# Values' high and low part as one stationary block of 128 columns, weights split at a later place, float32 products in eight steps instead of twenty-four

## The chip, the cores and the metric

The kernel runs on one core of a Trainium2 chip. The metric is device time in microseconds (us) of one launch, the median of the runs. Engines are called PE (TensorE's matmuls), PEld (its loads of the stationary operand), DVE (VectorE), ACT (ScalarE), POOL (GpSimd) and SP (the queue that issues the DMAs).

## The reference, cut to what matters

Local attention with a window of 32 and 32 global tokens, over 8 batches and 8 heads, then a two-layer network with 2048 hidden units over all 4352 rows. All of it is in float32.

```
s_g = scale * q_g @ k_all.T ;  out_g = softmax(s_g) @ v_all        # 32 global queries, all 544 keys
s_l = scale * [q_l @ k_g.T, mask(q_l @ k_l.T)]                     # 512 local queries, |i - j| <= 32
out_l = softmax(s_l) @ [v_g, v_l]
x = concat(out_g, out_l)  as 4352 rows of 512
h = x @ w_in ;  g = h * sigmoid(h) ;  out = g @ w_out              # w_in 512 x 2048, w_out 2048 x 512
```

The weights come as 64-bit floats and are turned to float32 on the chip.

## The kernel before

**Precision.** A float32 product is either given to PE as it is (one instruction, which the trace shows as two matmul records), or as three products of halves: a value x is split into a high part (a rounded copy in the format fp32r, made on ACT) and a low part (x minus the high part, made on DVE or POOL), and PE adds high x high, high x low and low x high in PSUM.

**Attention** runs in 128 steps: 8 batches b, 4 chunks c of 128 queries, 4 pairs of heads; step k does one pair for one chunk. A step loads queries and keys (`st_load`) and values (`st_vload`), splits them (`st_split`, `st_vsplit`), makes scores on PE and the softmax on DVE and ACT (`st_scores`), turns the probabilities by four PE transposes and splits them into `pt_hi` and `pt_lo` (`st_turn`), and multiplies them with the values into one PSUM bank `o` (`st_out`). Behind the 128 probabilities of the local queries `pt` holds 32 columns of the global queries (copied on POOL), so these matmuls are 160 wide for the first half a of the keys, and for the second half 128, except in the last chunk, where it is 160. For each of two heads u, a split step does six matmuls with a stationary block of 64 columns: pt_hi with vhi and with vlo for both halves a, then pt_lo with vhi for both. ACT and DVE then move the result out: xh and xl (high and low) for the local rows, and an addition to `acc` for the global rows. Steps k below KF use whole float32 (no splits, no DMA of the probabilities); below ND POOL makes the low parts of keys and values, from ND on DVE. Global scores and softmax of the next batch go in between (`g_*`): their 544 probabilities are brought by DMA into an fp32r tile (`g_move`), turned and kept in `pgt`.

**The network** runs in 12 blocks n of two or three tiles of 128 rows (SIZES). For each of 16 slices f of the hidden units: `first_layer` makes h, tanh and the split of g, `second_layer` of the slice before adds to the output tiles. Block 0 works in whole float32 while the weights are still being converted (`load_weights`: DMA, ACT line 179, DVE lines 181 and 182); `split_weights` makes their high parts on ACT (line 192) and low parts on POOL (line 193) for the blocks from 1 on.

**Order.** PE's order is the order of the code: a stream of attention parts with due times is advanced by `fill` between the network's matmuls, so the steps k = 8 to about 22 lie in block 0. The other engines and the DMA queue take an order that a list scheduler made; every engine works its list strictly in order. `keep_in_program_order` holds the first eight loads of weights (those of f = 0 to 3) at their place among the loads.

Of the kernel before, what the change touches and what calls it, by code (L numbers as in the profile page):

```python
# [39 lines left out]
ND = 28  # L40
KF = 24
GF = 2
KP = 12
SCRATCH = 8
LOOK = 5
FIRSTW, PACE, WAT = 2, 1.0, -1.5

# [11 lines left out]
def attention_moe_kernel(ctx: ExitStack, tc: tile.TileContext, qk0_in, qk_in, v_in, gqk, wts, out):  # L59
# [154 lines left out]
    def g_scores(b, p):  # L214
        did(("scores", b, p), *([("turn" if b <= GF else "move", b - 1, p // 2)] if b else []))
        rows = slice(QG * (p % 2), QG * (p % 2 + 1))
# [35 lines left out]
    def g_move(b, hh):  # L252
        did(("move", b, hh), ("soft", b, hh))
        if b < GF:
            return
        r0 = two.tile([P, 4 * P], F32R, tag="o", name=f"rg0_{b}_{hh}")
        r1 = two.tile([P, SG], F32R, tag="rg", name=f"rg1_{b}_{hh}")
        nc.sync.dma_start(out=r0.bitcast(F32), in_=pgs[hh][:, : 4 * P])
        nc.sync.dma_start(out=r1.bitcast(F32), in_=pgs[hh][:, 4 * P :])
        state["rg", hh] = r0, r1  # L260

    def g_turn(b, hh):
        whole = b < GF
        if whole:
            r0, r1, idt = pgs[hh], pgs[hh][:, 4 * P :], ident.bitcast(F32)
        else:
            (r0, r1), idt = state.pop(("rg", hh)), ident
        did(("turn", b, hh), ("turn", b, 0) if hh else ("last", b - 1))
        if hh == 0:
            state["pgt"] = work.tile([P, 5, H, SG], F32, tag="pgt", name=f"pgt{b}")  # L270
        pgt = state["pgt"]
# [5 lines left out]
        nc.scalar.copy(out=pgt[:, 0:4, hs, :], in_=tb.rearrange("p (t h q) -> p t h q", t=4, h=4))  # L277
# [15 lines left out]
    def st_vload(k, b, c, pr):  # L293
        if k < KF and k % 2:
            vraw = two.tile([P, 2, 2, D], F32, tag="vhi" if k % 4 == 1 else "vlo", name=f"vraw{k}")
# [20 lines left out]
    def st_vsplit(k, b, c, pr):  # L316
        if k < KF:
            return
        vraw = tiles.pop(("vraw", k))
        vhi = two.tile([P, 2, 2, D], F32R, tag="vhi", name=f"vhi{k}")  # L320
        vlo = two.tile([P, 2, 2, D], F32R, tag="vlo", name=f"vlo{k}")
        nc.scalar.copy(out=vhi, in_=vraw)
        (nc.gpsimd if k < ND else nc.vector).tensor_tensor(
            out=vlo, in0=vraw, in1=vhi.bitcast(F32), op=ALU.subtract)
        tiles["v", k] = vhi, vlo

# [41 lines left out]
    def st_turn(k, b, c, pr):  # L368
# [7 lines left out]
        for i in range(4):  # L376
# [3 lines left out]
            nc.tensor.transpose(t[:, i * P : (i + 1) * P].bitcast(F32R), rr[:, i * P : (i + 1) * P], ident)  # L380
        t4 = t.rearrange("p (u a q) -> p u a q", u=2, a=2)
        if whole:
            pt = tiles["pt", k] = pt_whole(k)
            if c == NC - 1:
                nc.gpsimd.memset(pt[:, :, 1, P:], 0.0)
            nc.scalar.copy(out=pt[:, :, :, :P], in_=t4)
        else:
            pt_hi, pt_lo = pt_tiles(k)
            nc.scalar.copy(out=pt_hi[:, :, :, :P], in_=t4)
            nc.vector.tensor_tensor(out=pt_lo[:, :, :, :P], in0=t4, in1=pt_hi[:, :, :, :P].bitcast(F32),  # L390
                                    op=ALU.subtract)
        did(("last", b) if (c, pr) == (NC - 1, NPR - 1) else k, ("turn", b, pr // 2))
        pgt = state["pgt"]
        for a in range(2 if c == NC - 1 else 1):
            n = P if a == 0 else SG
            g = pgt[:n, c + a, 2 * pr : 2 * pr + 2, :]
            if whole:
                nc.gpsimd.tensor_copy(out=pt[:n, :, a, P:], in_=g)
                continue
            nc.gpsimd.tensor_copy(out=pt_hi[:n, :, a, P:], in_=g)  # L400
            nc.gpsimd.tensor_tensor(out=pt_lo[:n, :, a, P:], in0=g, in1=pt_hi[:n, :, a, P:].bitcast(F32),
                                    op=ALU.subtract)

    def st_out(k, b, c, pr, t):
# [4 lines left out]
        if whole:  # L409
            vraw, pt_f = tiles.pop(("vraw", k)), tiles.pop(("pt", k))  # L410
        else:
            vhi, vlo = tiles.pop(("v", k))
            pt_hi, pt_lo = pt_tiles(k)
        o = attbank("o", f"o{k}")
        wide = P + SG
        for u in range(2):
            if whole:
                terms = [(vraw, pt_f, a) for a in range(2)]
            else:
                terms = [(v, pt_hi, a) for a in range(2) for v in (vhi, vlo)] + [(vhi, pt_lo, a) for a in range(2)]  # L420
            for i, (v, pt, a) in enumerate(terms):
                m = wide if a == 0 or c == NC - 1 else P
                nc.tensor.matmul(o[:D, u * wide : u * wide + m], v[:, a, u, :], pt[:, u, a, :m],  # L423
                                 start=(i == 0), stop=(i == len(terms) - 1))
        g0 = SG * (b % 4)
        for u in range(2):
            rows = slice(D * u, D * (u + 1))
            src = o[:D, u * wide : u * wide + P]
            if n == 0 and u == 0:
                nc.scalar.copy(out=xh[rows, pr, sl], in_=src)  # L430
            elif n == 0:
                nc.vector.tensor_copy(out=xh[rows, pr, sl], in_=src)
            else:
                nc.scalar.copy(out=xh[rows, pr, sl], in_=src)  # L434
                nc.vector.tensor_tensor(out=xl[rows, pr, sl], in0=src, in1=xh[rows, pr, sl].bitcast(F32),  # L435
                                        op=ALU.subtract)
            gsrc = o[:D, u * wide + P : (u + 1) * wide]
            gdst = acc[rows, pr, g0 : g0 + SG]
            if c == 0:
                nc.vector.tensor_copy(out=gdst, in_=gsrc)  # L440
            else:
                nc.vector.tensor_tensor(out=gdst, in0=gsrc, in1=gdst, op=ALU.add)

# [135 lines left out]
    def second_layer(n, f, gh, gl):  # L579
# [3 lines left out]
        for i, o in enumerate(outs[n]):  # L583
# [7 lines left out]
            fill(1)  # L591
        if n == 0:
            split_weights(f)
        if f == NF - 1:
# [11 lines left out]
    for n in range(len(SIZES)):  # L606
        for f in range(NF):
# [81 lines left out]
```

## Time and profile before

| | |
|---|---|
| time, median of 3 runs | 1088.51 us (1087.3 to 1088.69) |
| the profiled execution's own time | 1086.34 us |
| its span | 1084.6 us |
| busy: PE, PEld, DVE, ACT, POOL | 97%, 86%, 67%, 64%, 14% |
| matmul records, instructions in all | 6568, 20466 |
| mean granted clock of TensorE | 0.989 of full |

Matmuls overlap in the trace: a record of a 384-wide one is 0.34 us long, but the next begins 0.17 us after it. What a matmul costs in a full queue is therefore read from start to start, and the row behind a run of short ones is read with it.

### The profile page before, as it was taken

To read this page: it belongs to the slowest core of one execution; us is meant where nothing else is said; L and a number is where in the kernel's file an instruction comes from. 1 tells how busy PE (TensorE), PEld (TensorE's weight loads), DVE (VectorE), ACT (ScalarE), POOL (GpSimd) and SP (SyncE) were. 2 spreads that over 40 slices of the span, in tenths; PEclk is the share of its full clock that TensorE was granted. 3 is DMA by queue.
4 is the path that set the end of the run, shared out by engine and by line. 5 is a ranking of instruction groups with operands and counts; after the bars stand their busy time and mean duration, and the time that the engine had idled before them with its cause. 6 is when DMAs were issued, how large, how long until landed. Compare 5 with 4: busy or idle time off the path is not lost.

```text
span 1084.6 us, 20466 instructions
## 1 busy us (share of the span) xinstructions
PE 1053.5 (97%) x6568; PEld 934.9 (86%) x6568; DVE 727.4 (67%) x2367; ACT 693.0 (64%) x1845; POOL 146.5 (14%) x360
## 2 busy tenths in 40 slices
PE   6878999999999999999999999999999999999998
PEld 4645778989999999999999999998999999999997
DVE  5974355777677777666777877786778867753322
ACT  7875456767677766656766766776677776653232
POOL 3123542111100110000110100001000111000000
PEclk8989999999999999999999999999999999999999
DMA  9961112343334333332433433443344433310000
GB/s 351 380 189 59 57 59 76 119 146 125 111 112 142 124 107 115 116 115 82 140 110 122 149 111 109 138 135 108 111 141 125 141 114 112 112 60 20 1 30 20
DMA packets 69611, 127.29 MB, mean 117 GB/s; under 512 B 9344, under 2 KB 29312, under 8 KB 69504
## 3 DMA queue, kind: packets, MB, share of 16 engines
q1 hardware_dynamic: 69504, 125.99, 36.1%
q8 instruction: 52, 0.85, 0.3%
q14 instruction: 55, 0.45, 0.1%
HBM read 86.44 MB, written 8.91 MB: 88 GB/s over the span
## 4 chain that ended last, share of the span: by engine, by line
PE 93%; ACT 3%; DVE 2%; issue 1%; DMA 1%; ACTq 0%; DVEq 0%
PE h L563 33%; PE out L588 12%; PE out L590 11%; PE out L589 11%; PE o L423 10%; PE s L345 6%; PE t L380 3%; PE h L557 2%; PE out L586 2%; PE t L378 1%; DMA raw_w<-in_wts_dram 1%; PE gs L226 1%; PE gs L228 1%; ACT w_hi L192 1%; ACT w L179 1%
## 5 line engine op out<-in xcount | busy, mean ns | idle before, releaser
L563 PE MATMUL h<-xh,w_hi 128*128 128x384 f32 (+1 forms) x704 | 236.8, 336 | 0.0
L563 PE MATMUL h<-xh,w_lo 128*128 128x384 f32 (+1 forms) x704 | 233.5, 332 | 0.0
L563 PE MATMUL h<-xl,w_hi 128*128 128x384 f32 (+1 forms) x704 | 233.1, 331 | 0.0
L569 ACT ACTIVATE t<-h 128x384 f32<-128x384 f32 (+1 forms) x192 | 90.7, 472 | 207.3 <-PE h L563 189.4
L588 PE MATMUL out<-w_hi,gh 128*128 128x512 f32 x512 | 210.6, 411 | 0.0
L590 PE MATMUL out<-w_hi,gl 128*128 128x512 f32 x512 | 201.3, 393 | 0.0
L589 PE MATMUL out<-w_lo,gh 128*128 128x512 f32 x512 | 200.3, 391 | 0.0
L571 DVE SCALAR_TENSOR_TENSOR t<-t,h 128x384 f32<-128x384 f32 (+1 forms) x176 | 95.2, 541 | 132.6 <-ACT t L569 131.9
L563 PEld LDWEIGHTS h<-xl,w_hi 128*128 128x128 f32 x704 | 132.6, 188 | 5.4 <-issue 0.5
L563 PEld LDWEIGHTS h<-xh,w_hi 128*128 128x128 f32 x704 | 132.5, 188 | 5.4 <-issue 0.7
L400 POOL CAST pt_hi<-pgt 128x64 fp32r<-128x64 f32 (+1 forms) x132 | 39.1, 308 | 724.4 <-PE o L423 706.1
L563 PEld LDWEIGHTS h<-xh,w_lo 128*128 128x128 f32 x704 | 132.3, 188 | 0.0
L576 DVE TENSOR_TENSOR gl<-t,gh 128x384 fp32r<-128x384 f32 (+1 forms) x176 | 96.8, 550 | 46.6 <-PE out L590 42.5
L349 DVE CUSTOM_DVE_ANT_0 probs<-s,mask 128x224 f32<-128x224 f32 x244 | 85.0, 384 | 62.0 <-PE s L345 61.4
L353 ACT ACTIVATE probs<-probs,st 128x224 f32<-128x224 f32 x244 | 115.7, 475 | 11.2 <-DVE st L349 10.5
L590 PEld LDWEIGHTS out<-w_hi,gl 128*128 128x128 f32 x512 | 96.1, 188 | 22.3 <-DVE gl L576 0.3
L589 PEld LDWEIGHTS out<-w_lo,gh 128*128 128x128 f32 x512 | 97.0, 189 | 10.5
L588 PEld LDWEIGHTS out<-w_hi,gh 128*128 128x128 f32 x512 | 96.4, 188 | 10.6 <-ACT gh L575 0.4
L575 ACT CAST gh<-t 128x384 fp32r<-128x384 f32 (+1 forms) x176 | 88.3, 501 | 21.8 <-DVE t L571 17.3
L434 ACT CAST xh<-o 64x128 fp32r<-64x128 f32 x240 | 61.3, 256 | 42.5 <-PE o L423 29.4
L312 ACT CAST qk<-raw 128x704 fp32r<-128x704 f32 x100 | 78.2, 782 | 15.9 <-PE s L345 15.6
L435 DVE TENSOR_TENSOR xl<-o,xh 64x128 fp32r<-64x128 f32 x240 | 67.3, 280 | 30.9 <-ACT xh L434 27.4
(117 smaller groups left out, 1937.3 us busy)
## 6 DMA issues: line engine op xcount, KB each, us to landing
raw<-in_qk_dram SPq DMA_DIRECT2D x100, 352.0 KB, 3.0
rr<-probs SPq DMA_DIRECT2D x104, 256.0 KB, 2.3
raw_w<-in_wts_dram SPq DMA_DIRECT2D x32, 512.0 KB, 6.3
vraw<-in_v_dram SPq DMA_DIRECT2D x128, 128.0 KB, 2.4
raw_g<-in_gqk_dram SPq DMA_DIRECT2D x32, 304.0 KB, 2.9
out_dram<-o SPq DMA_DIRECT2D x32, 256.0 KB, 2.3
raw<-in_qk_dram SPq DMA_DIRECT2D x28, 240.0 KB, 4.8
rg<-pg SPq DMA_DIRECT2D x12, 256.0 KB, 2.4
```

The source lines that it names most:

```text
L312: nc.scalar.copy(out=qk, in_=raw)
L349: nc.vector.tensor_tensor_reduce(out=p[:, u, :W], in0=s[:, u * W : (u + 1) * W], in1=mask_of[c], scale=-SCALE, scalar=3.0e38, op0=ALU.add, ...
L353: nc.scalar.activation(p[:, u, :W], p[:, u, :W], AF.Exp, bias=st[:, u : u + 1], scale=-1.0, accum_out=st[:, 2 + u : 3 + u])
L423: nc.tensor.matmul(o[:D, u * wide : u * wide + m], v[:, a, u, :], pt[:, u, a, :m], start=(i == 0), stop=(i == len(terms) - 1))
L563: nc.tensor.matmul(h[:, :nt], wt, x[:, c, :nt], start=(i == 0), stop=(i == 3 * NCC - 1))
L569: nc.scalar.activation(t[:, :nt], h[:, :nt], AF.Tanh, scale=0.5)
L571: nc.vector.scalar_tensor_tensor(out=out[:, :nt], in0=t[:, :nt], scalar=1.0, in1=h[:, :nt], op0=ALU.add, op1=ALU.mult)
L575: nc.scalar.copy(out=gh[:, :nt], in_=t[:, :nt])
L576: nc.vector.tensor_tensor(out=gl[:, :nt], in0=t[:, :nt], in1=gh[:, :nt].bitcast(F32), op=ALU.subtract)
L588: nc.tensor.matmul(o, gh[:, sl], wh, start=(f == 0), stop=False)
L589: nc.tensor.matmul(o, gh[:, sl], wl, start=False, stop=False)
L590: nc.tensor.matmul(o, gl[:, sl], wh, start=False, stop=(f == NF - 1))
```

## The change

What it does, part by part. In a split step vhi and vlo become the two halves of one tile `vv`, so that one stationary block of 128 columns (vhi then vlo) is multiplied with pt_hi; the product lands in 128 partitions, high part in the first 64 and low part in the others. A step does eight matmuls in place of twelve. ACT copies the upper 64 partitions to a tile `xs`, DVE adds the lower 64, for each u; then ACT and DVE make xh and xl over 128 partitions in one instruction each, and POOL adds the global rows to `acc`. KF goes from 24 to 8: steps 8 to 23 are split steps now. The weights are no longer split after each slice of block 0 but by a count: the first at slice 7 of block 0, then one for each 0.75 slice. FIRSTW goes from 2 to 4: four instead of six halves of weights are asked for ahead of block 0. The last 32 probabilities of the global queries are turned as float32 straight from `pgs` (no second DMA) into two small tiles `pgh` and `pgl`.

```
-KF = 24
+KF = 8
+SPLIT0, SPLITS = 7, 0.75
-FIRSTW, PACE, WAT = 2, 1.0, -1.5
+FIRSTW, PACE, WAT = 4, 1.0, -1.5
...
         tb = attbank("s", f"gu{b}_{hh}")
-        nc.tensor.transpose(tb[:SG, :P] if whole else tb[:SG, :P].bitcast(F32R), r1, idt)
-        nc.scalar.copy(out=pgt[:SG, 4, hs, :], in_=tb[:SG, :P].rearrange("p (h q) -> p h q", h=4))
+        nc.tensor.transpose(tb[:SG, :P], pgs[hh][:, 4 * P :], ident.bitcast(F32))
+        for i in range(2):
+            rows, src = slice(SG * (2 * hh + i), SG * (2 * hh + i + 1)), tb[:SG, QG * i : QG * (i + 1)]
+            nc.scalar.copy(out=pgh[rows, :], in_=src)
+            nc.vector.tensor_tensor(out=pgl[rows, :], in0=src, in1=pgh[rows, :].bitcast(F32), op=ALU.subtract)
...
-        vhi = two.tile([P, 2, 2, D], F32R, tag="vhi", name=f"vhi{k}")
-        vlo = two.tile([P, 2, 2, D], F32R, tag="vlo", name=f"vlo{k}")
+        vv = two.tile([P, 2, 2, 2, D], F32R, tag="vv", name=f"vv{k}")
+        vhi, vlo = vv[:, :, :, 0, :], vv[:, :, :, 1, :]
...
         for u in range(2):
-                terms = [(v, pt_hi, a) for a in range(2) for v in (vhi, vlo)] + [(vhi, pt_lo, a) for a in range(2)]
...
+                nc.tensor.matmul(o[:, at], vv[:, a, u].rearrange("p t d -> p (t d)"), pt_hi[:, u, a, :m],
+                                 start=(a == 0), stop=(a == 1))
+                nc.tensor.matmul(o[:D, at], vv[:, a, u, 0], pt_lo[:, u, a, :m], start=False, stop=(a == 1),
+                                 skip_group_check=(a == 1))
...
-                nc.scalar.copy(out=xh[rows, pr, sl], in_=src)
-                nc.vector.tensor_tensor(out=xl[rows, pr, sl], in0=src, in1=xh[rows, pr, sl].bitcast(F32),
-                                        op=ALU.subtract)
...
-                nc.vector.tensor_tensor(out=gdst, in0=gsrc, in1=gdst, op=ALU.add)
+            nc.scalar.copy(out=xs[rows, :], in_=o[D:, at])
+            nc.vector.tensor_tensor(out=xs[rows, :], in0=o[:D, at], in1=xs[rows, :], op=ALU.add)
+        nc.scalar.copy(out=xh[:, pr, sl], in_=xs[:, :P])
+        nc.vector.tensor_tensor(out=xl[:, pr, sl], in0=xs[:, :P], in1=xh[:, pr, sl].bitcast(F32), op=ALU.subtract)
+        if c == 0:
+            nc.gpsimd.tensor_copy(out=gdst, in_=xs[:, P:])
+        else:
+            nc.gpsimd.tensor_tensor(out=gdst, in0=xs[:, P:], in1=gdst, op=ALU.add)
...
-        if n == 0:
-            split_weights(f)
...
+            while len(w_hi) < NF and SPLIT0 + SPLITS * len(w_hi) <= NF * n + f:
+                split_weights(len(w_hi))
             g = first_layer(n, f)
```

**PE, the values of step 30.** Before, twelve matmuls into 64 partitions (a name's first number is the step, `x2` stands for two rows):

```order
L423 MATMUL o30_2489<-pt_hi_1795,vhi30_2383 64x160
L423 MATMUL o30_2489<-pt_hi_1795,vlo30_2384 64x160
L423 MATMUL o30_2489<-pt_hi_1795,vhi30_2383 64x160
L423 MATMUL o30_2489<-pt_hi_1795,vlo30_2384 64x160
L423 MATMUL o30_2489<-pt_lo_1797,vhi30_2383 64x160 x2
```

These are the six of head u = 0, and the same six follow for u = 1. Now there are four for each head:

```order
L430 MATMUL o30_2801<-pt_hi_555,vv30_2701 128x160
L432 MATMUL o30_2801<-pt_lo_557,vv30_2701 64x160
L430 MATMUL o30_2801<-pt_hi_555,vv30_2701 128x160
L432 MATMUL o30_2801<-pt_lo_557,vv30_2701 64x160
L430 MATMUL o30_2801<-pt_hi_555,vv30_2701 128x160
```

The two with vlo are gone, and the blocks of 128 and of 64 columns alternate; PE's order around them is the same as before.

**POOL, in block 0, from the global rows of step 12 to those of step 13**, as it is now (`w_lo5` is the low part of the weights of slice 5, `klo` and `vv` are low parts of keys and values, `acc` the sum of the global rows):

```order
L458 TENSOR_TENSOR acc_125<-xs12_1016,acc_125 128x32
L315 TENSOR_TENSOR klo16_1164<-raw16_1093,qk16_1163 128x480
L194 TENSOR_TENSOR w_lo5_1379<-w5_630,w_hi5_1378 128x512 x2
L400 CAST pt_hi_555<-pgt0_202 128x2x32
L406 COPY pt_hi_555<-pgh0_203 32x2x32
L406 COPY pt_lo_557<-pgl0_204 32x2x32
L328 TENSOR_TENSOR vv15_1207<-vraw15_1086,vv15_1207 128x4x64
L194 TENSOR_TENSOR w_lo6_1450<-w6_697,w_hi6_1449 128x512 x2
L315 TENSOR_TENSOR klo17_1249<-raw17_1179,qk17_1248 128x480
L401 TENSOR_TENSOR pt_lo_557<-pgt0_202,pt_hi_555 128x2x32
L458 TENSOR_TENSOR acc_125<-xs13_1105,acc_125 128x32
```

Before, POOL's list in this stretch had the weights and small copies for `pt` alone:

```order
L193 TENSOR_TENSOR w_lo4_877<-w4_545,w_hi4_876 128x512 x2
L385 MEMSET pt13_975 128x2x32
L398 COPY pt13_975<-pgt0_208 128x2x32
L398 COPY pt13_975<-pgt0_208 32x2x32
L385 MEMSET pt14_1043 128x2x32
```

So the low parts of keys and values of steps 8 to 23 now stand between the weights, and the splits of the weights are still in block 0.

**ACT, ahead of the first tanh of block 0** (`t0_0`), as it is now: the turn of step 8 and conversions of weights 2, 3 and 6 stand directly before it.

```order
L314 CAST qk11_690<-raw11_628 128x480
L362 ACTIVATE probs1__117<-probs1__117,st9_524 128x224
L180 ACTIVATE w2_563<-raw_w2_0_564 128x512
L180 ACTIVATE w2_563<-raw_w2_512_569 128x512
L193 CAST w_hi2_1192<-w2_563 128x512
L180 ACTIVATE w3_574<-raw_w3_0_575 128x512
L193 CAST w_hi2_1192<-w2_563 128x512
L193 CAST w_hi3_1290<-w3_574 128x512
L180 ACTIVATE w3_574<-raw_w3_512_580 128x512
L397 CAST pt_hi_555<-t8_550 128x4x128
```

Three rows follow (a cast of w3 and two conversions of w6) before `t0_0`. Before, the rows ahead of it were these:

```order
L353 ACTIVATE probs1__117,st9_506<-probs1__117,st9_506 128x224
L430 COPY x_0_299<-o7_515 64x128
L353 ACTIVATE probs1__117,st9_506<-probs1__117,st9_506 128x224
L386 COPY pt8_531<-t8_526 128x4x128
L179 ACTIVATE w12_1015<-raw_w12_0_1016 128x512
L569 ACTIVATE t0_0_561<-h0_0_556 128x256
```

Counted over the two whole lists, 18 conversions (line 179) and 6 casts of weights (line 192) stood ahead of `t0_0` before, and 22 and 12 stand there now, with 4 casts of queries and keys and 2 of values that were not there. The transpose of step 8 needs its probabilities by DMA now, which is issued after the loads of the weights of slices 2 and 3.

## Rows read from the trace of the kernel before

**Rows 1.** Windows: from:to, length, busy of PE, PEld, DVE, ACT, POOL, clock, DMA share, GB/s
```profile
40.00:60.00 20.00, 15.53 (x83) 11.54 (x84) 17.37 (x60) 17.07 (x45) 1.58 (x4) 0.99 0.92 331
...
140.00:160.00 20.00, 20.00 (x97) 14.76 (x95) 11.92 (x38) 9.88 (x28) 9.28 (x10) 1.00 0.16 45
...
300.00:400.00 100.00, 99.99 (x667) 91.88 (x666) 76.26 (x250) 70.76 (x190) 10.77 (x34) 1.00 0.40 126
```

**Rows 2.** Waits of PE, whole span: us in total, times, longest
```profile
PE o L423 <- issue: 6.6, 5, 3.2
...
PE gs L226 <- DVE acc L442: 3.3, 1, 3.3
PE o L423 <- ACT pg L231: 2.7, 1, 2.7
```

**Rows 3.** Timeline of PE, a split step's twelve value matmuls: start, length
```profile
326.47 0.24 PE L423 MATMUL o<-pt_hi,vhi 128*64 128x160 f32 x1
...
327.28 0.45 PE L588 MATMUL out<-w_hi,gh 128*128 128x512 f32 x1
327.57 0.39 PE L589 MATMUL out<-w_lo,gh 128*128 128x512 f32 x1
327.80 0.39 PE L590 MATMUL out<-w_hi,gl 128*128 128x512 f32 x1
```

**Rows 4.** Timeline of PE, four transposes with 128 stationary columns, and what follows
```profile
608.59 0.46 PE L380 MATMUL t<-ident,rr 128*128 128x128 f32 x4
608.88 0.46 PE L588 MATMUL out<-w_hi,gh 128*128 128x512 f32 x1
609.19 0.39 PE L589 MATMUL out<-w_lo,gh 128*128 128x512 f32 x1
```

**Rows 5.** Timeline of PE, four score matmuls of 224 with 128 stationary columns
```profile
328.03 0.27 PE L345 MATMUL s<-qk 128*128 128x224 f32 x1
...
328.46 0.35 PE L563 MATMUL h<-xh,w_hi 128*128 128x384 f32 x1
```

**Rows 6.** Timeline of PE, a float32 step's values (step 23) and what follows
```profile
182.01 1.19 PE L423 MATMUL o<-pt,vraw 128*64 128x160 f32 x8
183.13 0.37 PE L345 MATMUL s<-qk 128*128 128x224 f32 x1
183.34 0.27 PE L345 MATMUL s<-klo,qk 128*128 128x224 f32 x1
```

**Rows 7.** Timeline of PE, the values of steps 12 and 18 in block 0
```profile
100.04 1.27 PE L423 MATMUL o<-pt,vraw 128*64 128x160 f32 x8 [0.51 <-issue]
...
144.19 1.19 PE L423 MATMUL o<-pt,vraw 128*64 128x160 f32 x8
```

**Rows 8.** Groups by line: POOL's, count, busy us, mean ns, idle before
```profile
L193 POOL TENSOR_TENSOR w_lo<-w,w_hi 128x512 fp32r<-128x512 f32 x32 | 41.1, 1304 | 47.5 <-PE out L586 29.6 <-ACT w_hi L192 17.8
L400 POOL CAST pt_hi<-pgt 128x64 fp32r<-128x64 f32 (+1 forms) x132 | 39.1, 308 | 724.4 <-PE o L423 706.1 <-ACT probs L353 18.1 <-ACT probs L357 0.2
L310 POOL TENSOR_TENSOR klo<-raw,qk 128x480 fp32r<-128x480 f32 x4 | 4.9, 1214 | 11.4 <-ACT qk L309 11.4
L323 POOL TENSOR_TENSOR vlo<-vraw,vhi 128x256 fp32r<-128x256 f32 x4 | 3.3, 818 | 2.6 <-ACT vhi L322 2.6
```

**Rows 9.** Groups by line: ACT's and DVE's moves of a step's result, and the weights' conversion
```profile
L435 DVE TENSOR_TENSOR xl<-o,xh 64x128 fp32r<-64x128 f32 x240 | 67.3, 280 | 30.9 <-ACT xh L434 27.4 <-PE out L586 0.4
L434 ACT CAST xh<-o 64x128 fp32r<-64x128 f32 x240 | 61.3, 256 | 42.5 <-PE o L423 29.4 <-DVE acc L442 4.1 <-DVE acc L440 4.0
L442 DVE TENSOR_TENSOR acc<-o,acc 64x32 f32<-64x32 f32 x192 | 33.3, 173 | 0.2
L179 ACT ACTIVATE w<-raw_w 128x512 f32<-128x512 f32 x32 | 21.3, 667 | 3.4 <-DMA raw_w<-in_wts_dram 3.2
L192 ACT CAST w_hi<-w 128x512 fp32r<-128x512 f32 x32 | 18.5, 614 | 4.8 <-DVE w L182 3.5 <-PE s L345 1.3
```

**Rows 10.** Timeline of ACT, the first tanh of block 0
```profile
49.96 0.38 ACT L569 ACTIVATE t<-h 128x256 f32<-128x256 f32 x1 [0.43 <-PE h L557]
```

More of the change, by code (lines that the diff above doesn't have):

```diff
@@ L214, in g_scores @@
     def g_scores(b, p):
-        did(("scores", b, p), *([("turn" if b <= GF else "move", b - 1, p // 2)] if b else []))
+        did(("scores", b, p), *([("turn", b - 1, p // 2)] if b else []))
         rows = slice(QG * (p % 2), QG * (p % 2 + 1))
@@ L256, in g_move @@
         r0 = two.tile([P, 4 * P], F32R, tag="o", name=f"rg0_{b}_{hh}")
-        r1 = two.tile([P, SG], F32R, tag="rg", name=f"rg1_{b}_{hh}")
         nc.sync.dma_start(out=r0.bitcast(F32), in_=pgs[hh][:, : 4 * P])
-        nc.sync.dma_start(out=r1.bitcast(F32), in_=pgs[hh][:, 4 * P :])
-        state["rg", hh] = r0, r1
+        state["rg", hh] = r0
     def g_turn(b, hh):
@@ L294, in st_vload @@
         if k < KF and k % 2:
-            vraw = two.tile([P, 2, 2, D], F32, tag="vhi" if k % 4 == 1 else "vlo", name=f"vraw{k}")
+            vraw = two.tile([P, 2, 2, 2, D], F32, tag="vv", name=f"vraw{k}")[:, 0]
         else:
@@ L415, in st_out @@
         wide = P + SG
+        gdst = acc[:, pr, SG * (b % 4) : SG * (b % 4 + 1)]
         for u in range(2):
-            if whole:
-                terms = [(vraw, pt_f, a) for a in range(2)]
-            else:
-                terms = [(v, pt_hi, a) for a in range(2) for v in (vhi, vlo)] + [(vhi, pt_lo, a) for a in range(2)]
-            for i, (v, pt, a) in enumerate(terms):
-                m = wide if a == 0 or c == NC - 1 else P
-                nc.tensor.matmul(o[:D, u * wide : u * wide + m], v[:, a, u, :], pt[:, u, a, :m],
-                                 start=(i == 0), stop=(i == len(terms) - 1))
@@ L425, in st_out @@
-        g0 = SG * (b % 4)
+            for a in range(2):
+                m = wide if a == 0 or c == NC - 1 else P
+                at = slice(u * wide, u * wide + m)
+                if whole:
+                    nc.tensor.matmul(o[:D, at], vraw[:, a, u, :], pt_f[:, u, a, :m], start=(a == 0), stop=(a == 1))
+                    continue
+                nc.tensor.matmul(o[:, at], vv[:, a, u].rearrange("p t d -> p (t d)"), pt_hi[:, u, a, :m],
+                                 start=(a == 0), stop=(a == 1))
+                nc.tensor.matmul(o[:D, at], vv[:, a, u, 0], pt_lo[:, u, a, :m], start=False, stop=(a == 1),
+                                 skip_group_check=(a == 1))
@@ new lines, in st_out @@
+        if n == 0:
+            for u in range(2):
+                rows = slice(D * u, D * (u + 1))
+                src, gsrc = o[:D, u * wide : u * wide + P], o[:D, u * wide + P : (u + 1) * wide]
+                if u == 0:
+                    nc.scalar.copy(out=xh[rows, pr, sl], in_=src)
+                else:
+                    nc.vector.tensor_copy(out=xh[rows, pr, sl], in_=src)
+                if c == 0:
+                    nc.vector.tensor_copy(out=gdst[rows, :], in_=gsrc)
+                else:
+                    nc.vector.tensor_tensor(out=gdst[rows, :], in0=gsrc, in1=gdst[rows, :], op=ALU.add)
+            return
@@ L426, in st_out @@
+        xs = work.tile([P, wide], F32, tag="xs", name=f"xs{k}")
         for u in range(2):
+            at = slice(u * wide, (u + 1) * wide)
             rows = slice(D * u, D * (u + 1))
-            src = o[:D, u * wide : u * wide + P]
-            if n == 0 and u == 0:
-                nc.scalar.copy(out=xh[rows, pr, sl], in_=src)
[L431 to L434, printed above, removed]
-                nc.vector.tensor_tensor(out=xl[rows, pr, sl], in0=src, in1=xh[rows, pr, sl].bitcast(F32),
-                                        op=ALU.subtract)
```

57 lines of the change are left out of this document (28 added, 29 removed).

## The prediction

> **What bounds the kernel now.** I read the windows first [rows 1]. In block 0's second half and in the middle PE has no gap: it is busy for 20.00 of 20 us and for 99.99 of 100, at full clock, while DVE is busy 76% and ACT 71% in the middle. There the time is PE's own work, and whatever is taken from PE comes off the end, as long as nobody else becomes late. At the start it is different: between 40 and 60 us PE is busy 15.5 of 20, DVE 17.4 and ACT 17.1, and the DMA engines are 92% full. That is the stage in which the weights arrive and are converted. The waits of PE [rows 2] lie nearly all in it: 6.6 us in which value matmuls wait for something the profile doesn't name, 3.3 us behind a DVE addition that holds the bank `o`, 2.7 us behind ACT. Then I read PE's timeline from start to start, since the records overlap.
>
> **Values, 104 steps that were split before.** The twelve matmuls begin at 326.47, the next matmul at 327.28, so 0.81 us [rows 3]. The matmul behind them then needs 0.29 where the one after it needs 0.23: 0.06 us of the run comes due there. Together 0.87 us, or 73 ns each. Eight instead of twelve at the same price would be 0.58. But four of the eight now have a stationary block of 128 columns. The nearest row is the four transposes, 128 columns stationary and 128 moving [rows 4]: 0.29 us to the next matmul, which then takes 0.31 instead of 0.23, so 0.37 us, or 92 ns each. So a step is 4 x 92 + 4 x 73 = 0.66 us and saves 0.21; 104 steps save 22 us. The bounds: if the wider block costs nothing, 0.87 - 0.58 = 0.29 a step, 30 us; if it costs as much as a score matmul with 128 stationary and 224 moving columns, 0.43 us for four or 108 ns each [rows 5], then 4 x 108 + 4 x 73 = 0.72, 0.15 a step, 15 us. I take the transposes, because their moving side is as short as here.
>
> The Trainium skill, page "TensorE: Matmul & The Clock Gate", section "LDWEIGHTS (loading the stationary operand)", says that a load takes the number of stationary columns divided by 1.2 GHz, whatever the rows: 107 ns for 128 columns and 53 ns for 64. By it alone the four wide ones would cost 107 ns each and the saving would be near 15 us, an estimate from that page. The transposes' 92 ns do not agree with it, the scores' 108 ns would.
>
> **Moving the result.** Before, a step has two ACT casts of 256 ns, two DVE subtractions of 280 and two additions of 173 [rows 9]. Now there are two ACT copies and two DVE additions of 64 x 160, an ACT cast and a DVE subtraction of 128 x 128, and a small POOL addition. Taking each as the nearest row, ACT goes from 0.51 to 0.77 us and DVE from 0.91 to 0.84, or a little more since 160 is wider than 128. For ACT that is 0.26 us a step in steps of some 8 us, 3% more on 71% [rows 1]: hidden, PE does not wait for ACT there. The bank `o` was passed from ACT to DVE to ACT to DVE before and is now, so its release costs nothing new. If that cover is gone, the price is the rival below.
>
> **Steps 8 to 23.** A float32 step's values take 1.12 us to the next matmul, which takes 0.21 where its like take 0.11 [rows 6, 5]: 1.22 us. As a split step it is 0.66: 0.56 less. The transposes and scores are about equal in both forms; I put 0.6 on the whole. Twelve of these steps (12 to 23) begin at 100 us or later [rows 7], where PE is the bound: at most 7 us. But POOL gets new work. With the rows of POOL [rows 8], from the global rows of step 12 to those of step 18 its list now holds nine pairs of weights' low parts (9 x 2.61), seven of keys (7 x 1.21), six of values (6 x 0.82) and 30 small operations of 0.31 at most: 23.5 + 8.5 + 4.9 + 9.3 = 46 us, perhaps 43 as many of the small ones are smaller than the row. PE took 144.19 - 100.04 = 44.2 us for the same six steps [rows 7] and would now want 40.6. So POOL holds this stretch at about what it was, and only steps 18 to 23, where two pairs of weights are left, give their 0.6 each: 4 us. I take 4; bounds 0 and 7.
>
> **The start.** Ahead of the first tanh of block 0 ACT now has 4 more conversions of weights (667 ns), 6 more casts of weights (614 ns) [rows 9], and 6 casts of keys and values that are new, bounded by those 614 ns: 2.7 + 3.7 + 3.7 = 10 us more on an engine that has no room there [rows 1]. The weights' part, 6.4 us, is not new work, only earlier: all 32 conversions and casts are done by about the same place of block 0, so it comes back there. What stays is the new casts, 3 us. Also late: the transpose of step 8 now waits for a DMA that is issued behind four loads of weights, and in the in-order list of ACT the first tanh stands behind it. I put the start at 3 us later; bounds: 10 us (nothing comes back), and 3 us earlier (two of the waits of [rows 2] go).
>
> The later split of weights changes nothing by itself: the scheduler still puts the high parts as early as before, and the low parts are done before block 1 needs them. One transpose per half batch as float32, and twelve DMAs less, are below what can be told.
>
> **Sum.** -22 - 4 + 3 = -23 us. From the profiled execution's own 1086.3 that gives 1063; the median of the runs stands 2 us above that execution, so about 1065; I say 1064.
>
> **Rivals.**
> - *The wide load binds.* The blocks of 128 columns are loaded more slowly than the short moving side runs, at 108 ns as in [rows 5]: -15 - 4 + 3 = -16 us, 1072. For it: no row shows a wide load behind a narrow one, and the scores are the dearest that there is; against: their moving side is longer than here, and the transposes take 92 ns. The page of the Trainium skill named above gives the same. 12%.
> - *POOL and the weights hold the start longer.* The DMAs of the probabilities of steps 8 to 11 stand in the one load queue behind loads of weights that wait for buffers, and each transpose waits; the start's 10 us stay and block 0 gains nothing: -22 + 10 = -12, 1076. For it: the order of the queue. Against: in the old run PE waits there anyway, for the same weights. 10%.
> - *More than thought.* The wide block costs nothing, POOL keeps up, the waits of 3.3 and 2.7 us go: -30 - 7 - 3 = -40 us, 1048. 12%.
> - *Slower.* One ACT list holds the copies of `o`, and its second copy waits for DVE's first addition. Behind it stand the tanh and the cast of g, for which the second layer waits. If that costs PE 0.22 us in each of 120 steps, the 26 us of the values and of block 0 are gone; at 0.35 us it is 42 - 23 = 19 us more, 1108. For it: DVE is 76% busy, so the addition queues. Against: the old chain has the same alternation, and PE waits for none of it between 300 and 400 us. 4%.
> - *No change*, where two of these meet half-way: 2%.
>
> **How the numbers follow.** The forecast as summed, 1053 to 1071 with the bounds of its three terms moved singly, has 60%. The range 1050 to 1077 takes in it, the wide load, most of the slow start and about a third of the case of more. 0.2% is 2 us, about what a measurement of this kernel can tell from no change: faster 94%, same 2%, slower 4%.
>
> **What the changed profile would show.** In the middle, PE still without a gap; eight value matmuls taking 0.6 to 0.66 us to the next one, with 60 to 75 ns behind a block of 64 columns and up to 92 ahead of one of 128. In block 0, POOL busy more than 9 of 10 us between steps 12 and 18, with PE waiting for `pt_lo` or for the low part of the values. The first tanh of block 0 near 58 us instead of 50 [rows 10], with most of these 8 us won back by step 12. I am wrong if PE shows waits for ACT or DVE in each step behind 200 us, or if the values' run is as long as before.

## The result and the profile after

The changed kernel takes **1093.5 us** (median; 1091.8 to 1093.9), the one before 1088.5 beside it: ratio 1.0044, 95% interval 1.0028 to 1.006. It is slower; the prediction said 1064 and 94% for faster. One of its five executions took 3509.7 us, three times the others, and is left out of the range and the ratio. The profiled execution has a span of 1091.6 us, 7.1 more than before's. First the page's span and engine shares:

```profile
span 1091.6 us, 20153 instructions
PE 1036.8 (95%) x6184; PEld 923.3 (85%) x6184; DVE 768.1 (70%) x2295; ACT 750.9 (69%) x2013; POOL 225.5 (21%) x528
```

The windows, columns as in [rows 1]:

```profile
40.00:60.00 20.00, 10.71 (x55) 8.68 (x53) 12.57 (x39) 12.88 (x32) 7.07 (x12) 0.67 0.59 197
...
120.00:140.00 20.00, 16.49 (x91) 12.07 (x91) 14.37 (x37) 12.15 (x37) 18.16 (x25) 1.00 0.30 94
140.00:160.00 20.00, 16.96 (x87) 12.53 (x86) 12.88 (x32) 10.97 (x33) 14.85 (x21) 0.91 0.25 76
...
300.00:400.00 100.00, 99.75 (x624) 91.70 (x624) 78.36 (x242) 75.36 (x205) 16.07 (x47) 1.00 0.41 125
```

In the middle PE still has no gap. The stage that changed is the start: between 40 and 60 us every engine is *less* busy than in [rows 1] except POOL, and the DMA engines moved 197 GB/s instead of 331. The next view says what PE waits for. The waits of PE, whole span, columns as in [rows 2]:

```profile
PE t L385 <- DMA rr<-probs__116: 11.7, 1, 11.7
PE gs L227 <- DVE xs L452: 6.2, 2, 3.1
PE o L426 <- issue: 4.8, 4, 2.3
PE s L350 <- DVE pgl L285: 4.3, 3, 3.0
```

One wait is 11.7 us long. On the timeline of PE (start, length, in brackets the idle time before) it is the transposes of step 8:

```profile
46.23 0.54 PE L350 MATMUL s<-qk 128*128 128x224 f32 x1
46.57 0.41 PE L350 MATMUL s<-klo,qk 128*128 128x224 f32 x1
46.78 0.41 PE L350 MATMUL s<-qk,klo 128*128 128x224 f32 x1
...
49.42 0.35 PE L350 MATMUL s<-qk 128*128 128x224 f32 x1
...
49.72 0.28 PE L350 MATMUL s<-qk,klo 128*128 128x224 f32 x1
49.83 0.27 PE L350 MATMUL s<-qk 128*128 128x224 f32 x1
...
50.81 1.17 PE L426 MATMUL o<-pt,vraw 128*64 128x160 f32 x8 [0.49 <-issue]
63.66 0.72 PE L385 MATMUL t<-ident,rr 128*128 128x128 f32 x4 [11.68 <-DMA rr<-probs__116]
64.18 2.03 PE L573 MATMUL h<-x,w 128*128 128x256 f32 x4
```

The reader should see the order: the scores of steps 8 and 9 (46.23 and 49.42), the values of step 7 (50.81), the transposes of step 8 (63.66), and only behind them the first slice of block 0 (64.18; the expectations below call the network's slices expert slices). That slice needs nothing of step 8, but it stands behind it on PE's list. The timeline of SP, the one queue from which loads and copies are issued:

```profile
44.62 0.33 SPq L172 DMA_DIRECT2D raw_w<-in_wts_dram  x1
49.10 0.33 SPq L303 DMA_DIRECT2D vraw<-in_v_dram  x1
...
52.34 2.14 SPq L172 DMA_DIRECT2D raw_w<-in_wts_dram  x4
54.60 0.70 SPq L370 DMA_DIRECT2D rr<-probs__116  x1
```

Between 44.95 and 49.10 SP issues nothing: its next load waits for the buffer that a values run of PE still reads. Then four halves of weights go out at once, 512 KB each, and the copy for step 8 goes out behind them at 54.60. The DMA view from 40 to 70 us says when it lands (KB each, us from issue):

```profile
raw_w<-in_wts_dram SPq DMA_DIRECT2D x10, 512.0 KB, 5.5
...
rr<-probs__116 SPq DMA_DIRECT2D x1, 256.0 KB, 8.9
```

54.6 + 8.9 = 63.5, and PE goes on at 63.66. (From 100 us on, the copies land in 2.3 us by the median.)

A second cost stands beside the waits: TensorE's granted clock. In these traces it is at one of two levels, 1.2 GHz (0.50 in the windows) and 2.4 GHz (1.00). PE had stood still since 51.98 when the clock fell at 54.80, and it stayed low to 68.5, so the transposes of step 8 and the first slice ran at the lower level. Two windows, columns as in [rows 1]:

```profile
54.80:63.66 8.86, 0.00 (x1) 0.03 (x1) 3.88 (x8) 3.90 (x8) 1.30 (x2) 0.50 0.94 334
63.66:68.50 4.84, 4.84 (x16) 4.12 (x17) 2.82 (x5) 3.36 (x6) 0.00 (x0) 0.50 1.02 398
```

What the lower level costs can be seen in the scores on the timeline of PE above: at 46.57 and 46.78, with the clock at 0.50, two such matmuls begin 0.21 us apart; at 49.72 and 49.83, with the clock at 1.00, 0.11.

The values' run in the middle, timeline of PE, answers [rows 3]:

```profile
323.91 0.24 PE L430 MATMUL o<-pt_hi,vv 128*128 128x160 f32 x1
323.98 0.24 PE L432 MATMUL o<-pt_lo,vv 128*64 128x160 f32 x1
324.06 0.26 PE L430 MATMUL o<-pt_hi,vv 128*128 128x128 f32 x1
...
324.58 0.39 PE L579 MATMUL h<-xh,w_hi 128*128 128x384 f32 x1
324.81 0.34 PE L579 MATMUL h<-xl,w_hi 128*128 128x384 f32 x1
324.98 0.34 PE L579 MATMUL h<-xh,w_lo 128*128 128x384 f32 x1
```

From 323.91 to 324.58 is 0.67, and the next matmul takes 0.23 where its like take 0.17: 0.73 us against 0.87 before. The change gives 0.14 to 0.15 a step, not 0.21.

Where the time went is plainest from the first matmul of a slice, read off the traces of the runs, one execution of each (us later than in before):

```
slice (block, f)   (0,0)   (0,4)   (1,0)   (2,0)   (7,0)   end
changed           +16.5   +18.6   +15.4   +14.2    +9.6   +7.1
KF = 8 alone       +7.1   +12.0   +18.4   +16.0   +15.8  +17.4
FIRSTW = 4 alone    0.0    -2.1    -6.0    -6.0    -6.0   -4.4
late split alone   +0.3    -0.7    +3.4    +3.4    +3.2   +4.8
values, KF 24      +1.9    -5.1    -4.3    -3.4    -8.8  -10.5
KF = 9             +4.5    -0.4    +1.7    +0.5    -5.0   -6.4
KF = 12            -0.9    -5.9    -4.9    -6.1   -11.6  -13.3
```

The changed kernel loses 15 us by the end of block 0 and wins 8 back in the blocks behind. The three kernels with the old values part each lose 1.6 us between (7,0) and (8,0) that before's profiled execution did not lose: in each of them the clock is at 1.2 GHz for 3.4 us there, in before's never. So that execution is a fortunate one, as its 1086.3 beside the median says; the late split's is the slowest of its ten (1091.3, median 1089.5).

The stretch ahead of (1,0) can be taken apart with the same traces. PE is idle, or busy at 2.4 GHz, or busy at 1.2 GHz; the last is counted here as half work and half loss, an estimate from the score matmuls above.

```
us ahead of (1,0)     idle   lost to 1.2 GHz   PE's work    sum
before                24.4        11.0           119.4     154.9
changed               43.6        16.7           110.0     170.3
KF = 24, FIRSTW = 4   24.1         7.7           119.5     151.3
KF = 8 alone          48.5        13.5           111.2     173.3
FIRSTW = 4 alone      23.5         5.4           120.0     148.8
values, KF 24         24.6         6.2           119.7     150.5
KF = 9                36.7         7.7           112.3     156.6
KF = 12               29.3         6.6           114.0     150.0
```

That the work comes out alike in the table's four kernels with KF = 24 (before has 24 too) supports the halving. KF = 8 does take some 9 us of work off PE by the end of block 0, near the 0.6 that the prediction put on each of 16 steps; the changed kernel pays for them with 19 us of waiting and 6 us of clock. Over the changed kernel's executions the mean granted clock is 0.977 to 0.980, over those of the kernel before 0.986 to 0.994.

### The profile page after: what moved, and what is told of

The parts are those of the page before. It is cut to its first block, busy times and chain, and to the rows that moved or that the text cites. A ratio compares the mean times of both kernels' runs of the same rounds, so it can differ in the third digit from the quotient of the medians.

```text
span 1091.6 us, 20153 instructions
## 1 busy us (share of the span) xinstructions
PE 1036.8 (95%) x6184; PEld 923.3 (85%) x6184; DVE 768.1 (70%) x2295; ACT 750.9 (69%) x2013; POOL 225.5 (21%) x528
## 4 chain that ended last, share of the span: by engine, by line
PE 87%; ACT 4%; DVE 4%; DMA 2%; issue 2%; SPq 0%; POOL 0%; ACTq 0%; DVEq 0%
PE h L579 32%; PE out L604 11%; PE out L606 11%; PE out L605 11%; PE s L350 5%; PE o L430 4%; PE t L385 3%; PE o L432 3%; PE out L602 2%; PE h L573 2%; DMA rr<-probs__116 1%; ACT probs L358 1%; ACT w_hi L193 1%; DVE xl L454 1%; PE o L426 1%
## 5 line engine op out<-in xcount | busy, mean ns | idle before, releaser
L400 POOL CAST pt_hi<-pgt 128x64 fp32r<-128x64 f32 x120 | 39.6, 330 | 502.1 <-PE o L432 328.2
L430 PE MATMUL o<-pt_hi,vv 128*128 128x160 f32 x480 | 97.8, 272 | 4.2 <-ACT pg L232 1.9
L452 DVE TENSOR_TENSOR xs<-o,xs 64x160 f32<-64x160 f32 x240 | 75.7, 315 | 35.3 <-ACT xs L451 30.8
L430 PEld LDWEIGHTS o<-pt_hi,vv 128*128 128x128 f32 x480 | 89.6, 191 | 11.9 <-issue 5.2
```

The source lines that it names most:

```text
L430: nc.tensor.matmul(o[:, at], vv[:, a, u].rearrange("p t d -> p (t d)"), pt_hi[:, u, a, :m], start=(a == 0), stop=(a == 1))
L452: nc.vector.tensor_tensor(out=xs[rows, :], in0=o[:D, at], in1=xs[rows, :], op=ALU.add)
```

## The experiments

Medians of 4 to 10 executions, each with the kernel before beside it (1087.9 to 1088.6). In the first group theory A puts the loss on step 8's copy behind the weights' loads, which KF = 8 and FIRSTW = 4 make together; rival C puts it on KF = 8 alone.

**Group 1: which of the new constants?** KF = 24 and FIRSTW = 2 in the changed kernel, that is, the values' part, the global rows and the late split (with KF over 12 a float32 step in the last chunk needs its global rows cleared and added, and one past block 0 its result copied to `xs`):

```
-KF = 8
+KF = 24
-FIRSTW, PACE, WAT = 4, 1.0, -1.5
+FIRSTW, PACE, WAT = 2, 1.0, -1.5
...
+            if whole:
+                nc.scalar.copy(out=xs[rows, :], in_=o[:D, at])
+                continue
```

> The changed kernel with KF = 24 and FIRSTW = 2 again: what is left of the change is the 128-column block of values, the sum of the halves, the later split of weights and the global rows. Theory A (the loss is made ahead of block 0 by the float32 steps taken away together with the later request for weights): block 0 begins near 48 us as before, 104 steps save 0.15 us each, 16 us, of which some 4 go into new short gaps; about 1076. Rival B (the longer chain of a step's result or the late split cost as much as the block saves, everywhere): 1086 to 1090.

Measured 1076.0 (1073.9 to 1076.8), ratio 0.9886 (0.9868 to 0.9903). The other three are the kernel before with `KF = 8`, before with `FIRSTW = 4`, and the changed kernel with `FIRSTW = 2`, one line each.

> The kernel before with KF = 8 alone. Here the load list has step 8's probabilities ahead of the weights of slice 3, so theory A expects block 0's first matmul 4 to 8 us late, and 12 split steps behind it that are 0.35 us cheaper than in float32 (0.87 against 1.22): 1089 to 1093. Rival C (POOL's and ACT's added work of steps 8 to 23 is the whole loss, wherever the weights stand): the 16 us of the changed kernel's block 0 appear here too, about 1102.

Measured 1105.9, ratio 1.0162 (1.0143 to 1.0182). On the old kernel more than half of the loss comes behind the first slice: +7.1 us at (0,0), +18.4 at (1,0).

> The kernel before with FIRSTW = 4 alone. Theory A: with float32 steps nothing in step 8 waits for a DMA behind the weights, so the time moves by less than 3 us, 1087 to 1091. Rival D (weights of slices 2 and 3 asked for late are enough by themselves, the tanh stands behind them in the list of ACT): 8 to 12 us more, about 1098.

Measured 1082.2, ratio 0.9947 (0.9927 to 0.9967): a gain, all of it made in block 0. In the traces 5.6 of its 6.0 us are the clock (11.0 against 5.4 us lost to 1.2 GHz); the idle time hardly differs.

> The changed kernel with FIRSTW = 2 alone. Theory A: the 11.7 us in which PE waits for step 8's probabilities shrink to 3 or less, because only the probabilities' own loads stand ahead of them; 8 to 9 us less than the changed kernel, about 1085. Rival C: the start is as late as in the changed kernel, within 2 us of 1093.

Measured 1095.3, ratio 1.0067 (1.005 to 1.0084): no help. Timeline of PE in this run:

```profile
53.41 0.51 PE L385 MATMUL t<-ident,rr 128*128 128x128 f32 x4 [2.34 <-DMA rr<-probs__116]
...
63.17 0.31 PE L430 MATMUL o<-pt_hi,vv 128*128 128x160 f32 x1 [3.38 <-POOL klo L315]
...
67.17 2.04 PE L602 MATMUL out<-w,gh 128*128 128x512 f32 x2 [2.41 <-DVE gh L587]
...
75.57 1.14 PE L227 MATMUL gs<-raw_g 128*64 128x272 f32 x2 [4.78 <-DVE xs L452]
```

The 11.7 us wait has shrunk to 2.3 (the first slice starts at 53.8 instead of 64.2), and others have taken its place by (0,2), where the run is again 17.3 us behind. Theory A's half about FIRSTW falls. KF = 8 costs 17 us on the old kernel; the longest single wait was where the loss showed, not what it depended on.

**Group 2: which work of KF = 8, and the wide load.** First KF = 24 with FIRSTW = 4 kept:

> The changed kernel with KF back at 24; everything else of the change stays (128-column block, halves added, global rows, late split, FIRSTW = 4). Theory C (the loss is KF = 8, which costs some 17 us, and FIRSTW = 4 is worth some 5 us): 1093.5 - 17 - 5 against the run with FIRSTW = 2, that is about 1070, 1067 to 1074, ratio about 0.983. Rival (FIRSTW = 4 only helped because the weights were split early, so that with the late split it adds nothing): 1075 to 1077, like the run with KF = 24 and FIRSTW = 2. Rival (KF = 8 is innocent and only FIRSTW = 4 together with it costs): 1076 or above.

Measured 1078.5 (1074.4 to 1079.6). So KF = 8 costs the changed kernel 15.0 us, and FIRSTW = 4 adds nothing beside the rest. Next, steps 8 to 23 transposed in float32 without the copy, then the low parts on VectorE:

```
-KF = 8
+KF, KR = 8, 24
...
-        if k < KF:
+        if k < KR:
             tiles["p", k] = p.rearrange("p u j -> p (u j)")
...
```

> The changed kernel (KF = 8), but steps 8 to 23 transpose their probabilities in float32 straight from the tile that ScalarE and VectorE wrote, without the copy by DMA into rr; their scores and values stay split. Theory D (the way over the DMA queue in the open start and in block 0 is what KF = 8 costs): most of the 17 us comes back, 1076 to 1082. Theory P (the low parts of keys and values, which KF = 8 puts on GpSimd for 16 more steps, cost it): the same as the changed kernel, 1090 to 1096. Theory W (the split steps cost it by their number of instructions on all engines together, no one of them): a part, 1084 to 1090.

```
-        (nc.gpsimd if k < ND else nc.vector).tensor_tensor(
+        nc.vector.tensor_tensor(
             out=vlo, in0=vraw, in1=vhi.bitcast(F32), op=ALU.subtract)
...
```

(The two lines that make klo change in the same way.)

> The changed kernel (KF = 8) with the low parts of keys and values of steps 8 to 27 on VectorE instead of GpSimd (klo 1.2 us and vlo 0.8 us a step on GpSimd; less than half on VectorE). Theory P (GpSimd is what KF = 8 loads too much): 1076 to 1084. Theory D (the copies into rr) and theory W (all engines together): 1089 to 1097, since VectorE is as loaded in the start as GpSimd is.

Measured 1086.7 (-6.8) and 1087.9 (-5.6). Without the copy the first slice starts 5.5 us later than before's instead of 16.5, and PE then waits elsewhere. With the low parts on VectorE the start is nearly as late as ever (15.3 us), and most of the gain comes in block 0. Its waits:

```profile
PE t L385 <- DMA rr<-probs__116: 10.1, 1, 10.1
PE o L426 <- issue: 6.6, 5, 2.4
PE o L432 <- DVE pt_lo L398: 4.9, 4, 2.9
```

The fourth kernel loads 128 columns in all eight value matmuls, which adds vlo times pt_lo to the output:

```
-                nc.tensor.matmul(o[:D, at], vv[:, a, u, 0], pt_lo[:, u, a, :m], start=False, stop=(a == 1),
+                nc.tensor.matmul(o[:, at], vv[:, a, u].rearrange("p t d -> p (t d)"), pt_lo[:, u, a, :m], start=False, stop=(a == 1),
```

> The changed kernel with the 128-column block also in the four matmuls by pt_lo (64 columns there now), so that all eight matmuls of a values step load 128 columns and the output also takes in vlo times pt_lo, which the changed kernel leaves out. If a wide load sets the pace of such a run (0.73 us for four wide and four narrow ones now, that is 110 and 73 ns each): 8 x 110 = 0.88 us, 0.15 a step dearer in some 110 steps, +14 to +16 us, 1106 to 1110. If a run of eight is set by something else (the 192 columns that move, the eviction), nothing: 1092 to 1095.

Measured 1110.8, 17.3 more. Its timeline of PE:

```profile
327.88 0.24 PE L430 MATMUL o<-pt_hi,vv 128*128 128x160 f32 x1
...
328.60 0.27 PE L432 MATMUL o<-pt_lo,vv 128*128 128x128 f32 x1
328.71 0.39 PE L579 MATMUL h<-xh,w_hi 128*128 128x384 f32 x1
328.94 0.34 PE L579 MATMUL h<-xl,w_hi 128*128 128x384 f32 x1
```

0.83 to the next matmul and 0.06 behind: 0.89 us, 111 ns each. With 0.73 for four wide and four narrow, a narrow one is 71 ns. The loads of the stationary blocks, timeline of PEld in the same run:

```profile
327.99 0.19 PEld L430 LDWEIGHTS o<-pt_hi,vv 128*128 128x128 f32 x1
328.10 0.19 PEld L432 LDWEIGHTS o<-pt_lo,vv 128*128 128x128 f32 x1
328.21 0.19 PEld L430 LDWEIGHTS o<-pt_hi,vv 128*128 128x128 f32 x1
```

They begin 0.11 us apart all through the run, whether 160 or 128 columns move. So the width of the block sets the pace of these short matmuls, not their moving side. Columns loaded and partitions written are the same number here and were not tried apart.

**Group 3: do the two causes add, and what do the other parts bring?**

> The changed kernel (KF = 8) with both of the edits that helped in part: steps 8 to 23 transposed in float32 without the copy into rr, and the low parts of keys and values of steps 8 to 27 on VectorE. If the two costs are separate (the wait for rr in the start, GpSimd's load in block 0) they add: 1093.5 - 6.8 - 5.6 = 1081, 1079 to 1083, and what is left to the 1078 of KF = 24 is the split steps' other work. If they are one cost (each edit only loosens the same stretch), no more than the better of them: 1085 to 1088.

Measured 1087.4 (1084.3 to 1089.8): no better than either. That fits two ways to loosen the same stretch; some 9 us remain.

> The kernel before with the late split of the weights alone (SPLIT0 = 7, SPLITS = 0.75; FIRSTW = 2, KF = 24 and the values unchanged). The prediction's step (late split changes nothing by itself): 1088 to 1090, ratio 1.000. Theory L (the late split takes ScalarE's and GpSimd's weight work out of the first slices of block 0, where FIRSTW = 4 also gains, and is what the run with FIRSTW = 2 and KF = 24 gained there): 1083 to 1085, ratio about 0.995.

Measured 1089.5, ratio 1.0007 (0.9995 to 1.0019): the late split alone is nothing. Theory L falls, and the next run says the same.

The values' part with the global rows alone (KF = 24, FIRSTW = 2, weights split slice by slice in block 0), and the same with FIRSTW = 4:

```
-            while len(w_hi) < NF and SPLIT0 + SPLITS * len(w_hi) <= NF * n + f:
-                split_weights(len(w_hi))
...
+        if n == 0:
+            split_weights(f)
```

> The values part and the global rows alone: the changed kernel with KF = 24, FIRSTW = 2 and the weights split slice by slice in block 0 as before. Theory L (the late split brought the 4 to 5 us in block 0): the gain is that of the blocks behind alone, 0.15 us a step of the late steps less what new waits cost, -5 to -6 us, 1082 to 1084. If the values part made the gain in block 0 too: 1076 to 1078.

> As the run before it, but with FIRSTW = 4. Theory L' (FIRSTW = 4 and the late split are two ways to free the same stretch of block 0, worth 5 to 6 us each and no more together): 1076 to 1079, like the runs with KF = 24 and the late split. If the late split costs something beside FIRSTW = 4, which the early one does not: 1071 to 1074, the fastest of all.

Measured 1075.5 (1075.0 to 1076.3), ratio 0.9882 (0.9868 to 0.9897), and 1078.2 (1074.3 to 1078.3). So values and global rows are worth 13 us by themselves, 4 of them by the end of block 0. The waits of PE in the first of the two:

```profile
PE o L430 <- issue: 9.4, 8, 2.6
PE gt L278 <- DVE pg L251: 4.5, 1, 4.5
PE gs L227 <- DMA raw_g<-in_gqk_dram: 4.0, 1, 4.0
PE gt L278 <- issue: 3.3, 6, 2.0
```

The 3.3 us behind DVE's `acc` and the 2.7 us behind ACT's `pg` of [rows 2] are gone, but other waits have come: ahead of (1,0) PE is idle as long as before (24.6 us against 24.4). What is smaller is the time lost to 1.2 GHz, 6.2 us against 11.0, and that is the whole gain up to there in these two executions. No split step stands there yet; which part of the change brings it was not tried. FIRSTW = 4, worth 6 us alone and also by the clock, adds nothing here either.

**Group 4: which half of a split step, and which steps?** The two halves (KS bounds the float32 scores, KV the float32 transposes and values; the second kernel has 8, 24), and KF = 12 and 16:

```
-KF = 8
+KS, KV = 24, 8
```

> The changed kernel, but steps 8 to 23 take their scores in float32 from the loaded tile (no copy qk on ScalarE, no klo on GpSimd); their probabilities and values are split as in the changed kernel, with the copy into rr. If the scores' half costs most (klo is the longest single instruction that KF = 8 adds, 1.3 us on GpSimd, and every scores step stands behind it): 1078 to 1084. If the values' half with its copy costs most: 1088 to 1094.

> The changed kernel, but steps 8 to 23 transpose, turn and multiply values in float32 (no copy into rr, no pt_lo, no split of the values); their scores are split. If the values' half costs most: 1078 to 1084, that is well under the 1087 of the run that only left out the copy into rr. If the scores' half costs most: 1086 to 1092. If each half costs on its own, both this run and the one before it come to 1084 to 1087.

> The changed kernel with KF = 12: steps 8 to 11 in float32 too. If the start is what costs (steps 8 to 11 stand ahead of the first expert slice, where the changed kernel lost 14 of its 16 us): 1079 to 1084. If each split step beside block 0 costs the same (15 us in 16 steps, 0.95 each): 1093.5 - 4 x 0.95 = 1089 to 1091.

> The changed kernel with KF = 16: steps 8 to 15 in float32 too. If the start is what costs: 1077 to 1080, no dearer than KF = 24. If each split step costs the same: 1093.5 - 8 x 0.95 = 1085 to 1087.

Measured 1079.1, 1081.2, **1074.5** (1072.3 to 1076.6; ratio 0.9872, 0.9853 to 0.9891) and 1076.1 (1074.6 to 1076.5). Either half in float32 gives back 12 to 14 of 15 us, so the costs of the halves don't add: it takes both to make the loss. And the steps that matter are 8 to 11: with KF = 12 the loss is gone. Steps 12 to 23 as split steps gain 1 to 4 us (1074.5 against 1075.5 to 1078.5 in the four kernels with KF = 24 and the new values), which is not clear of the spread. The windows with KF = 12:

```profile
40.00:60.00 20.00, 17.67 (x93) 13.01 (x92) 14.94 (x51) 18.33 (x48) 5.45 (x8) 1.00 0.92 312
...
140.00:160.00 20.00, 19.57 (x108) 15.16 (x107) 14.07 (x41) 14.51 (x41) 15.36 (x23) 1.00 0.38 123
```

The start is as full as in [rows 1] again.

**Group 5: one step or four?** `KF = 9` and `KF = 10`:

> The changed kernel with KF = 9: step 8 alone in float32, so that the transposes ahead of the first expert slice no longer read a tile that comes by DMA; step 9's scores still stand ahead of it. If the one step whose whole chain stands ahead of the first slice carries the loss: 1075 to 1081. If the four steps carry it in equal shares: 1093.5 - 4.8 = 1087 to 1091. If what counts is that any split step begins in the start (its first klo, the clearing of pt_hi and pt_lo, the first copy): 1090 to 1094.

> The changed kernel with KF = 10: steps 8 and 9 in float32, so that no split step stands ahead of the first expert slice. If the place ahead of the first slice carries the loss: 1073 to 1077, as with KF = 12. If the four steps carry it in equal shares: 1093.5 - 9.6 = 1083 to 1085.

Measured 1081.4 (1080.2 to 1082.9) and 1084.0 (1081.2 to 1087.4). The waits of PE for a copy with KF = 9:

```profile
PE t L385 <- DMA rr<-probs__117: 1.8, 1, 1.8
```

The whole row by KF, all with FIRSTW = 4 and the late split:

```
KF          24       16       12       10        9        8
median  1078.5   1076.1   1074.5   1084.0   1081.4   1093.5
```

Step 8 alone carries 12 of the 19 us between KF = 8 and KF = 12; the copy of step 9, which is then the first, still takes 6.4 us to land, but the first slice no longer stands behind it. The other 7 us hang on steps 9 to 11, and ahead of (1,0) they are idle time of PE (36.7 us with KF = 9, 29.3 with KF = 12); step 9 shows no share of its own (KF = 10 is no faster than KF = 9, and its runs spread over 6 us).

## Why the prediction was wrong, by its own steps

**The failed step is the start**: "What stays is the new casts, 3 us ... I put the start at 3 us later; bounds: 10 us ...". The first slice started 16.5 us later, and 15.4 us were still missing at block 1. Of the 16.5, 15.3 are waiting (ahead of the first slice PE is idle for 29.0 us, before for 13.7) and 2.2 the lower clock; its work is 1.0 less. No term of the sum stood for the clock. I had the mechanism in hand, the transposes of step 8 behind a DMA behind four loads of weights, and priced it as instructions: so many casts on ACT. The price was that of a chain. Scores, softmax, copy and transposes of step 8 all come ahead of the first slice on PE; two lists that are worked in order meet there, PE's and SP's, and when SP's head waits, the weights behind it wait too: 197 GB/s instead of 331. POOL's list is not what makes the start late: with the low parts taken off it, the first slice is still 15.3 us late. The first tanh came at 67.96, where I said 58 [rows 10]:

```profile
67.96 0.38 ACT L585 ACTIVATE t<-h 128x256 f32<-128x256 f32 x1 [0.17 <-PE h L573]
```

The rival *POOL and the weights hold the start longer* named the right place and the wrong size (10 us), and it counted on the values' 22 us beside it. Its argument against, that PE waits there anyway for the same weights, is what the runs refute: with KF = 12 the same weights come and the first slice starts 0.9 us earlier than before's.

**Values, -22 us, was mis-sized.** The run measured 0.73, which is the rival *the wide load binds* (0.72, from the scores' 108 ns), not my 0.66 from the transposes' 92 ns; the run of eight wide blocks (111 ns each) shows that it is their width. The Trainium skill, page "TensorE: Matmul & The Clock Gate", section "LDWEIGHTS (loading the stationary operand)", has a load take its columns divided by 1.2 GHz, by which 128 columns would take 107 ns and 64 columns 53 (estimates from that page). These runs agree with it for the wide block (111 ns); the narrow ones go at 71. On the whole the part brought 13 us, 4 of them by the end of block 0. Of the 0.15 a step, some 0.1 reached the end: from (2,0) to (7,0), 56 steps, the kernel with values and KF = 24 gains 5.4 us. Summed from start to start, its value runs are 8.1 us shorter there and the network's 1680 matmuls 2.9 us longer.

**Steps 8 to 23, -4 us**: right for steps 18 to 23: from the values of step 18 to those of step 24 the changed kernel takes 43.3 us instead of 46.3, 3 us less where 6 x 0.6 was forecast. Not right for steps 12 to 18, which the forecast put level: from the values of step 12 to those of step 18 the changed kernel takes 47.4 us, the one before 44.2, so steps 12 to 23 together gave nothing. The windows of the two, changed and before:

```profile
113.18:160.56 47.38, 40.82 (x213) 29.58 (x213) 32.33 (x83) 28.44 (x84) 39.67 (x56) 0.96 0.25 79
...
100.04:144.19 44.15, 43.44 (x199) 30.80 (x199) 20.97 (x82) 21.11 (x64) 21.73 (x26) 1.00 0.17 49
```

POOL was busy 39.7 us there (43 forecast), that is 84% and not the more than 90% forecast, which it reached only between 120 and 140. PE was idle for 6.6 us instead of 0.7, and for 3.4 us at 1.2 GHz. Wrong for steps 8 to 11, by the 19 us between KF = 8 and KF = 12.

**The late split changes nothing**: right (1.0007). **Moving the result is hidden**: right; in the middle ACT rose from 70.76 to 75.36 of 100, and PE is busy 99.75 us of it. The rival *slower* put its price on ACT's list in every step; the kernel got slower by another road.

**FIRSTW = 4** had no term of its own. It gains 6 us alone and nothing (0 to 3 us of loss, within the spread) beside the new values, in whose traces the time lost to 1.2 GHz is as small already (6.2 us without it, 7.7 with it and the late split).

**Two slips in the working.** The waits of [rows 2] do not lie nearly all in the start: of the 6.6 us, 3.2 end at 74.3, and the 2.7 us behind ACT end at 89.1, both in block 0. And with one term moved at a time the sum's lower end is 1056, not 1053.

The sum from the runs: 1088.5 - 13 (values and global rows) + 0 to 3 (FIRSTW = 4) + 0 (late split) + 15 (KF = 8) = 1090.5 to 1093.5.

What stays open: which resource gives way first at steps 8 to 11 (copy, GpSimd and either half of the split each loosen it, and the waits that remain change their names), and what in steps 9 to 11 costs the other 7 us. The clock was not varied by itself: its share is worked out from one execution of each kernel. A second buffer for `rr`, and a list on PE with the first slice ahead of step 8, weren't tried.

## What to carry to other kernels

Price a step that moves ahead of a busy loop as a chain, from its first load to its last reader, and look what stands behind it on each in-order list; a sum of instruction times (3 us here, for 16.5) is only a lower bound. Then look at the clock behind each new wait: it carried some 6 us of this loss, and nearly all of the 6 us that `FIRSTW = 4` gained alone. When one long wait is removed and the time stays, its successors are the measure: vary the amount (here KF in single steps) instead of chasing the wait. Here a constant that was safe at 12 cost 19 us at 8, so sweep such a constant: KF = 12 with the rest of the change is 1.3% faster than the kernel before.

## What the runs showed of the hardware

With a short moving side (128 to 160 columns) a matmul whose stationary block has 128 columns takes 111 ns from start to start and one with 64 columns 71 ns; four transposes with 128 took 92 ns each [rows 4], so the two kinds of wide load do not cost the same.

Unexpected: in all 16 traced kernels with the new values part the second layer's matmuls by w_lo, the same instructions as before, take 232 ns from start to start (means over 240 of them between (2,0) and (7,0)), and 228 in before and the three kernels that have its values part. With the other matmuls of the network that is the 2.9 us above, and it eats some of the gain in the middle. The runs don't tell why.
